# ReLU-squared attention and token/channel mixer: the first batch's transposes move to other PSUM banks, one score tile moves to VectorE, and one pair of DMA transposes moves a round later

## The chip, the core and the metric

The kernel runs on one core of a Trainium2 chip. The metric is the device time of one execution in microseconds (us). The engines are TensorE (PE; its weight loads are PEld), VectorE (DVE), ScalarE (ACT), GpSimd (POOL) and SyncE (SP). In this kernel SP only issues DMAs, and POOL issues the loads, copies a few small things and builds one constant.

## The reference

For 8 batches, 12 heads, 448 tokens and a head width of 64:

```
scores = q @ k.T / 8
attn   = max(scores, 0)**2 / 448
x      = (attn @ v), heads side by side          # 8 x 448 x 768
h      = max(x.T @ w_tok1, 0) @ w_tok2           # over tokens, 448 -> 256 -> 448
u      = x + h.T
out    = u + max(u @ w_ch1, 0) @ w_ch2           # over channels, 768 -> 1536 -> 768
```

Inputs and output are float32. The kernel computes in bf16 with float32 sums.

## The kernel before

**The unit of work** is a group of four heads, numbered i = 0 to 23, three to a batch (`DB` = 3). For each group:

- `load_four` (L73) loads q, k and v; POOL's queue casts them to bf16.
- `transposes(i)` (L127) makes q and k head-major: 56 small transposes on PE into PSUM, then one or two copies to SBUF (`qkT`). With place "att" both halves lie in one slot of the score tiles' pool and are copied by one VectorE instruction of 1792 elements per partition (L152). With place "acc" they lie in the banks acc0 and acc1, with one copy of 896 elements each (L155).
- `scores(i, c)` (L159) for c = 0 to 6: four 64x64 matmuls into a score tile of 128 x 896 float32, then a ReLU on ScalarE (L174) that writes the bf16 tile `at`. The pool `ps_att` has two slots, so a score tile waits until the ReLU of the tile two before has read its slot.
- `square` (L178) squares waiting `at` tiles on VectorE (L181), all but the last `keep`.
- `values(i, cs)` (L183) multiplies the squared tiles with v into acc0 and acc1; `values_out` (L202) moves the sums to `xT`, half on VectorE (L211), half on ScalarE (L207) where `split` is set.
- `x_back(i)` (L223) transposes `xT` to `x_sb`: for i < 8 on PE and by a copy (L246), from i = 8 on by a DMA transpose on SP's queue (L228).
- `token1(i)` (L250) and `token2(i)` (L266) are the token mixer. With `early`, token2's results lie in the pool `ps_mm`, whose tag "bank" has two buffers that go round; then VectorE adds `xT` (L286) and writes `uT`.

The channel mixer follows by batches: `channel1` (L320), `channel2` (L358), whose result is added to `u_sb` on VectorE (L373) and stored from SP's queue (L385). `u_sb` is made by `u_back` (L303), two DMA transposes for each group on SP's queue (L309).

**The order is written out by hand.** Every engine runs its own instructions strictly in the order in which the program issues them, and waits are only put where data or buffers ask for them. PSUM is full: `ps_att` two slots of two banks each, acc0, acc1, and two "bank" buffers.

**The first batch** (L461 to L490) loops over i = 0, 1, 2 and within it over c = 0 to 6. Parts of the group before are laid between the score tiles: values of i-1 at c = 0, 1, 2, token2 of i-2 at c = 1 and 2, x_back of i-1 at c = 4 (into a "bank" buffer, copied by ScalarE), the transposes of the next group at c = 3 (i = 0) or c = 5 (into a score slot), values of i at c = 5 and 6, token1 of i-1 at c = 6. `keep_clock` (L431) issues matmuls on zeros into `warm_ps`, which was taken from "bank" at the very start, in i = 0 and in the first part of i = 1. There is no channel work yet to fill PE with.

**The second batch's first group** (i = 3, L494 to L523) is written out line by line and ends the first batch's last group: squares, values, scores, token2 of 1, x_back of 2, token1 of 2, and so on. From L526 on, all groups run in one loop in which `fill` (L410) lays channel work between the parts.

**u_back's order.** `u_later` (L297) holds the groups whose `uT` is done. At i = 7 the first three are issued (L574 to L577), held back by small POOL copies (`hold_back`, L314). At i = 8 the loop at L545 issues all groups below i - 1 = 7, that is 3, 4, 5 and 6: eight DMA transposes. At i = 9 `x_back(8)`, the first by DMA, comes ahead of `u_back(7)` in program order, and so in SP's queue.

Of the kernel before, what the change touches and what calls it, by code (L numbers as in the profile page):

```python
# [9 lines left out]
FP32 = mybir.dt.float32  # L10
BF16 = mybir.dt.bfloat16
AF = mybir.ActivationFunctionType
ALU = mybir.AluOpType
# [3 lines left out]
def kernel(  # L17
# [11 lines left out]
    nc = tc.nc  # L29

    B, H, S, D = q.shape
# [6 lines left out]
    DB = H // 4  # L38
# [17 lines left out]
    ps_acc = ctx.enter_context(tc.tile_pool(name="ps_acc", bufs=1, space=bass.MemoryType.PSUM))  # L56
    ps_mm = ctx.enter_context(tc.tile_pool(name="ps_mm", bufs=2, space=bass.MemoryType.PSUM))
# [69 lines left out]
    def transposes(i, place="acc", split=False):  # L127
        sb = attn.tile([128, 2, 2, S], BF16, name="qkT")
        if place == "att":
            both = ps_att.tile([128, 2, 1024], BF16, tag="att", name="qkT_ps")  # L130
            parts = [both[:, r] for r in range(2)]
        else:
            parts = [ps_acc.tile([128, 1024], BF16, tag=f"acc{r}", name="qkT_ps1") for r in range(2)]
        for w in (1, 0) if i == 0 else (0, 1):
            src = raws.pop((i, "qk"[w]))
            for c in range(QC):
                at = w * S + c * 64
                for r in range(2):
                    h = slice(64 * r, 64 * (r + 1))
                    for g in range(2):  # L140
                        nc.tensor.matmul(  # L141
                            parts[r][64 * g : 64 * (g + 1), at : at + 64],
                            lhsT=src[h, g, c, :],
                            rhs=ident[h, h],
                            is_transpose=True,
                            start=True,
                            stop=True,
                            skip_group_check=True,
                        )
        qkT[i] = sb  # L150
        if place == "att":
            nc.vector.tensor_copy(sb.rearrange("n r w t -> n r (w t)"), both[:, :, : 2 * S])  # L152
            return
        for r in range(2):
            (nc.scalar.copy if split and r == 0 else nc.vector.tensor_copy)(  # L155
                sb[:, r].rearrange("n w t -> n (w t)"), parts[r][:, : 2 * S]
            )

    def scores(i, c):  # L159
        sb = qkT[i]  # L160
        ps = ps_att.tile([128, 2, 512], FP32, tag="att", name="sc_ps")
        for r in range(2):
            for g in range(2):
                h = slice(64 * g, 64 * (g + 1))
                nc.tensor.matmul(  # L165
                    ps[64 * r : 64 * (r + 1), g, :S],
                    lhsT=sb[h, r, 1, c * 64 : (c + 1) * 64],
                    rhs=sb[h, r, 0, :],
                    start=True,
                    stop=True,  # L170
                    skip_group_check=True,
                )
        at = attn.tile([128, 2, S], BF16, name="at", bufs=12)
        nc.scalar.activation(at, ps[:, :, :S], AF.Relu)  # L174
        squares.append(at)
        at2[i, c] = at

    def square(keep=0):  # L178
        while len(squares) > keep:
            at = squares.pop(0)  # L180
            nc.vector.tensor_tensor(out=at, in0=at, in1=at, op=ALU.mult)  # L181
# [81 lines left out]
        nc.scalar.activation(r1, ps, AF.Relu)  # L263
        r1_tiles[i] = r1

    def token2(i, early=False, rs=(0, 1)):  # L266
        b, d = divmod(i, DB)
        if d == 0 and b % 2 == 0 and 0 in rs:
            uT_tiles[b // 2] = mix.tile([128, NP, 2 * S], BF16, name="uT_sb")
        r1 = r1_tiles[i]  # L270
        off = (b % 2) * S
        if early:
            parts = {r: ps_mm.tile([128, 512], FP32, tag="bank", name="h_ps1") for r in rs}
        else:
            parts = {r: ps_acc.tile([128, 512], FP32, tag=f"acc{r}", name="h_ps") for r in rs}
        for r in rs:
            for j in range(JC):
                nc.tensor.matmul(  # L278
                    parts[r][:, :S],
                    lhsT=r1[:, j, r * 128 : (r + 1) * 128],  # L280
                    rhs=wt2[:, j, :],
                    start=(j == 0),
                    stop=(j == JC - 1),
                )
        for r in rs:
            nc.vector.tensor_tensor(  # L286
                out=uT_tiles[b // 2][:, 2 * d + r, off : off + S],
                in0=parts[r][:, :S],
                in1=xT[b % 2][:, 2 * d + r, :S],
                op=ALU.add,  # L290
            )
        if 1 in rs:
            u_later.append(i)
# [3 lines left out]
    u_later = []  # L297
# [130 lines left out]
    for i in range(9):  # L428
        nc.tensor.matmul(warm_ps, lhsT=warm[:, :128], rhs=warm, start=True, stop=True)

    def keep_clock(n):  # L431

        for m in range(n):
            for r in range(2):
                h = slice(64 * r, 64 * (r + 1))
                nc.tensor.matmul(
                    warm_ps[h, :], lhsT=warm[h, :64], rhs=warm[h, :],
                    start=True, stop=True, skip_group_check=True,
                )
# [15 lines left out]
    load_four(3, "v")  # L455


    keep_clock(2)
    transposes(0, "acc", split=True)
    keep_clock(3)  # L460
    for i in range(DB):  # L461
        for c in range(QC):
            scores(i, c)
            if i == 0:
                keep_clock(0 if c == 3 else 1 if c > 4 else 2)
            if i == 1 and c < 4:
                keep_clock(1)
            square(keep=1)
            if c < 3 and i > 0:
                values(i - 1, (4 + c,))  # L470
                if c == 2:
                    values_out(i - 1, split=True)
            if c in (1, 2) and i > 1:
                token2(i - 2, early=True, rs=(c - 1,))
            if c == 3 and i == 0:
                transposes(1, "att")
            if c == 4 and i > 0:
                x_back(i - 1, copy=nc.scalar.copy)
            if c == 5:
                if i > 0:  # L480
                    transposes(i + 1, "att")
                values(i, (0, 1))
            if c == 6:
                if i > 0:
                    token1(i - 1)
                values(i, (2, 3))
        if i == 1:
            load_four(4)
        if i == 2:
            load_four(5)  # L490
            load_wc1(1, 2)


    i = DB  # L494
    square()
    values(i - 1, (4, 5, 6))
    values_out(i - 1, split=True)
    scores(i, 0)
    token2(i - 2, early=True)
    x_back(i - 1, place="acc0")  # L500
    scores(i, 1)
    token1(i - 1)
    square(keep=1)
# [22 lines left out]
    for i in range(DB + 1, ND + 2):  # L526
        slow = i <= 2 * DB
        if i == 2 * DB + 1:
            rate[0] = (EC * C1 + NT * C2) / DB
        if i < ND:  # L530
            scores(i, 0)
            scores(i, 1)
        if 0 <= i - 1 < ND:
            values(i - 1, range(QC))
            values_out(i - 1)
        if i < ND:
            scores(i, 2)
        if i - 1 < XDMA:
            fill(1 / 3, least=1)
        if 0 <= i - 1 < ND:  # L540
            x_back(i - 1)
        if i > 2 * DB + 1:
            if i == 2 * DB + 2:
                hold_back(1, x_tiles[i - 1][:1, 0, 0, :1])
            while u_later and u_later[0] < i - 1:  # L545
                u_back(u_later.pop(0))
        if i + PRE < ND:
            if i - 1 >= XDMA:
                nc.gpsimd.tensor_copy(gate, x_tiles[i - 1][:1, 1, 3, 127:])  # L549
            load_four(i + PRE)  # L550
        if i == 5:
            load_wc2(1, 2)
        square()
        if i - 1 >= XDMA:
            fill(1 / 3)
        if i < ND:
            scores(i, 3)
            scores(i, 4)
        if i + 1 < ND:
            transposes(i + 1)  # L560
        square()
        if not slow:
            fill(2 / 9)
        if 0 <= i - 1 < ND:
            token1(i - 1)
        fill(1 / 3 if slow else 1 / 9, least=1)
        if i < ND:
            scores(i, 5)
            scores(i, 6)
        if 0 <= i - 1 < ND:  # L570
            token2(i - 1)
            if (i - 1) % DB == DB - 1:
                channel_work((i - 1) // DB)
            if i == 2 * DB + 1:  # L574
                hold_back(0, uT_tiles[1][:1, 0, :1])
                for _ in range(DB):
                    u_back(u_later.pop(0))  # L577
        square()
        fill(1 / 3, least=1 if slow else 0)
# [32 lines left out]
```

## Time and profile before

| | |
|---|---|
| median of 7 runs | 381.34 us (379.6 to 382.7) |
| the profiled execution's own time | 381.02 us |
| its span, first to last instruction | 379.2 us |
| PE busy | 364.9 us (96%) |
| ACT busy | 213.4 us (56%) |
| DVE busy | 206.5 us (54%) |
| POOL busy | 100.3 us (26%) |
| granted TensorE clock, mean | 1.000 |

A row of a timeline holds the start, the length, the engine, the line in the kernel, the operation, what it writes and reads, how many instructions are merged, and, in square brackets, how long the engine had sat idle and what ended that. Lengths of neighbours on one engine overlap a little: on VectorE and ScalarE the next instruction starts about 0.1 us before the end of the one before. A merged group of matmuls is as long as from its first start to its last modelled end; the next group starts before that. The chain of waits is followed back from a last instruction through whatever released each step.

### The profile page before, as it was taken

Reading aid. Unit: us, or ns where it says so; the run is one execution under the profiler, and the core shown is the slowest. Engines: PE = TensorE matmul, PEld = TensorE weight load, DVE = VectorE, ACT = ScalarE, POOL = GpSimd, SP = SyncE. Lnnn points to the kernel's source line nnn. Section 1 sums busy time; section 2 is a strip of 40 time slices with the busy share of each in tenths; the row PEclk is TensorE's granted clock in tenths of the full one; section 3 lists DMA queues with packets and bytes.
Section 4 is the critical chain, followed back from the end, with each engine's and each line's share of the span. In section 5 each row is a group of like instructions: output and inputs, shape, how many; then the busy total and the mean of one; then the engine's idle time right before and its main releaser. Section 6 shows DMA issues by size and latency. Waiting matters only on the chain.

```text
span 379.2 us, 10082 instructions
## 1 busy us (share of the span) xinstructions
PE 364.9 (96%) x4335; PEld 200.6 (53%) x4335; DVE 206.5 (54%) x371; ACT 213.4 (56%) x297; POOL 100.3 (26%) x186
## 2 busy tenths in 40 slices
PE   7878999999979999999999999999999999999995
PEld 3444455555545554555555654555545654555563
DVE  2886688764566575465555664466555664121021
ACT  4996888877434457755676247654676446412400
POOL 8976347312312321421312304303300000000000
PEclk9999999999999999999999999999999999999999
DMA  8999999913998866947745798648451434333024
GB/s 150 119 161 197 177 206 188 165 25 74 110 170 154 149 143 113 112 77 153 130 86 74 128 163 132 102 70 171 87 106 23 90 93 92 57 69 85 0 61 107
DMA packets 69325, 43.30 MB, mean 114 GB/s; under 512 B 43360, under 2 KB 65824, under 8 KB 69280
## 3 DMA queue, kind: packets, MB, share of 16 engines
q0 software_dynamic: 24416, 21.47, 40.0%
q1 hardware_dynamic: 44560, 20.75, 25.8%
q8 instruction: 34, 0.56, 0.6%
q10 hardware_dynamic: 304, 0.43, 0.4%
q14 instruction: 11, 0.09, 0.1%
HBM read 43.38 MB, written 11.01 MB: 143 GB/s over the span
## 4 chain that ended last, share of the span: by engine, by line
PE 87%; DVE 4%; DMA 3%; ACT 3%; POOL 2%; issue 1%; POOLq 0%; ACTq 0%; SPq 0%
PE m_ps L327 28%; PE m_ps L366 28%; PE sc_ps L165 9%; PE acc_ps L193 8%; PE t_ps L255 6%; PE h_ps L278 5%; DMA x_sb<-xT 3%; PE qkT_ps L141 2%; ACT at L174 2%; DVE uT_sb L286 1%; DVE at L181 1%; POOL q_raw L83 1%; PE m_ps L345 1%; DMA wt<-in_moe_w_tok_dram 1%; PE x_ps L237 1%
## 5 line engine op out<-in xcount | busy, mean ns | idle before, releaser
L174 ACT ACTIVATE at<-sc_ps 128x896 bf16<-128x896 f32 x168 | 145.1, 921 | 59.3 <-PE sc_ps L165 59.1
L327 PE MATMUL m_ps<-uT_sb,wc 128*128 128x448 bf16 x564 | 115.6, 353 | 0.2 <-DVE uT_sb L286 0.2
L366 PE MATMUL m_ps<-wc,r_sb 128*128 128x384 bf16 x672 | 115.2, 326 | 0.0
L181 DVE TENSOR_TENSOR at<-at 128x896 bf16<-128x896 bf16 x168 | 97.3, 622 | 7.1 <-ACT at L174 7.1
L366 PEld LDWEIGHTS <-r_sb 128*128 128x128 bf16 x672 | 64.3, 98 | 45.6 <-issue 3.9
L334 ACT ACTIVATE r_sb<-m_ps 128x448 bf16<-128x448 f32 x94 | 51.1, 543 | 60.1 <-PE m_ps L327 59.8
L327 PEld LDWEIGHTS <-wc 128*128 128x128 bf16 x564 | 53.3, 98 | 49.8 <-issue 4.3
L373 DVE TENSOR_TENSOR out_sb<-m_ps,u_sb 128x384 f32<-128x384 f32 x56 | 31.1, 556 | 62.0 <-PE m_ps L366 61.0
L165 PE MATMUL sc_ps<-qkT 64*64 64x448 bf16 x672 | 52.7, 360 | 2.9 <-ACT at L174 2.3
L286 DVE TENSOR_TENSOR uT_sb<-h_ps,xT 128x448 bf16<-128x448 f32 x48 | 27.8, 619 | 39.4 <-PE h_ps L278 39.3
L211 DVE TENSOR_SCALAR xT<-acc_ps 128x448 bf16<-128x448 f32 x45 | 26.1, 620 | 34.9 <-PE acc_ps L193 34.9
L193 PE MATMUL acc_ps<-at,v_raw 64*64 64x448 bf16 x672 | 38.6, 349 | 0.0
L549 POOL COPY gate<-x_sb 1x1 bf16<-1x1 bf16 x12 | 2.4, 199 | 127.4 <-DMA x_sb<-xT 127.4
L83 POOL DMA_DIRECT2D q_raw<-in_q_dram x48 | 29.0, 615 | 17.4 <-DMA wc<-in_moe_w_ch_dram 14.0
L83 POOL DMA_DIRECT2D v_raw<-in_v_dram x48 | 29.4, 637 | 10.4 <-DMA wc<-in_moe_w_ch_dram 5.2
L165 PEld LDWEIGHTS <-qkT 64*64 64x64 bf16 x672 | 15.6, 105 | 30.7 <-issue 26.6
L155 DVE COPY qkT<-qkT_ps 128x896 bf16<-128x896 bf16 x39 | 22.6, 619 | 14.6 <-PE qkT_ps L141 14.6
L83 POOL DMA_DIRECT2D k_raw<-in_k_dram x46 | 28.1, 632 | 1.4 <-DMA k_raw<-in_k_dram 0.9
L255 PE MATMUL t_ps<-x_sb,wt 128*128 128x256 bf16 x192 | 25.0, 273 | 3.3 <-DMA x_sb<-xT 2.5
L263 ACT ACTIVATE r_sb<-t_ps 128x512 bf16<-128x512 f32 x24 | 14.3, 597 | 21.8 <-PE t_ps L255 21.7
L193 PEld LDWEIGHTS <-v_raw 64*64 64x64 bf16 x672 | 20.2, 107 | 12.1 <-issue 0.8
L255 PEld LDWEIGHTS <-wt 128*128 128x128 bf16 x192 | 18.2, 98 | 9.1 <-DMA x_sb<-xT 3.4
(40 smaller groups left out, 125.4 us busy)
## 6 DMA issues: line engine op xcount, KB each, us to landing
out_dram<-out_sb SPq DMA_DIRECT2D x54, 192.0 KB, 3.5
q_raw<-in_q_dram POOLq DMA_DIRECT2D x48, 112.0 KB, 4.4
v_raw<-in_v_dram POOLq DMA_DIRECT2D x48, 112.0 KB, 5.6
k_raw<-in_k_dram POOLq DMA_DIRECT2D x46, 112.0 KB, 5.7
wc<-in_moe_w_ch_dram POOLq DMA_DIRECT2D x4, 1152.0 KB, 10.5
u_sb<-uT_sb SPq DMA_TRANSPOSE x48, 2.8
x_sb<-xT SPq DMA_TRANSPOSE x16, 3.3
k_first<-in_k_dram SPq DMA_DIRECT2D x1, 224.0 KB, 3.5
```

The costliest lines, as they stand in the source:

```text
L83: eng.dma_start(out=dst[64 * r : 64 * (r + 1)].rearrange("p g c d -> p g (c d)"), in_=src[b, h0 : h0 + 2].rearrange("g (p c) d -> p g (c d ...
L165: nc.tensor.matmul(ps[64 * r : 64 * (r + 1), g, :S], lhsT=sb[h, r, 1, c * 64 : (c + 1) * 64], rhs=sb[h, r, 0, :], start=True, stop=True, s ...
L174: nc.scalar.activation(at, ps[:, :, :S], AF.Relu)
L181: nc.vector.tensor_tensor(out=at, in0=at, in1=at, op=ALU.mult)
L193: nc.tensor.matmul(ps[r][64 * g : 64 * (g + 1), :S], lhsT=v_raw[h, g, c, :], rhs=at[h, g, :], start=(c == 0), stop=(c == QC - 1), skip_gro ...
L211: nc.vector.tensor_scalar(out=xT[b % 2][:, 2 * d + r, :S], in0=ps[r][:, :S], scalar1=float(alpha2), scalar2=None, op0=ALU.mult,)
L255: nc.tensor.matmul(ps[:, j, :], lhsT=wt1[:, c, j * 128 : (j + 1) * 128], rhs=x_sb[:, :, c, :], start=(c == 0), stop=(c == 3),)
L286: nc.vector.tensor_tensor(out=uT_tiles[b // 2][:, 2 * d + r, off : off + S], in0=parts[r][:, :S], in1=xT[b % 2][:, 2 * d + r, :S], op=ALU.add,
L327: nc.tensor.matmul(ps[:, :S], lhsT=wc1[:, g, e * 128 : (e + 1) * 128], rhs=uT[:, g, off : off + S], start=(g == 0), stop=(g == CC - 1),)
L334: nc.scalar.activation(r2[:, e, off : off + S], ps[:, :S], AF.Relu)
L366: nc.tensor.matmul(ps[:, :HN], lhsT=r2[:, e, t * 128 : (t + 1) * 128], rhs=wc2[:, e, cols], start=(e == 0), stop=(e == EC - 1),)
L373: nc.vector.tensor_tensor(out=o[:, cols].rearrange("n (g d) -> n g d", d=128), in0=ps[:, :HN].rearrange("n (g d) -> n g d", d=128), in1=u_ ...
```

## The change

1. `transposes(1)`, `transposes(2)` and `transposes(3)` use two "bank" buffers of `ps_mm` instead of one score slot; their copy becomes two copies of 896 elements on VectorE (the line of L155) instead of one of 1792 (L152). `transposes(4)` stays in a score slot.
2. After `transposes(1)`, `warm_ps` is taken anew from "bank", since its old buffer went to the transposes.
3. Score tile (0, 2) gets its ReLU from VectorE instead of ScalarE (a maximum with 0), and is then squared on VectorE as all are.
4. Values of a group come one score tile later: chunks 0 and 1 at c = 6 instead of c = 5, then (2, 3), (4, 5) and (6) at c = 0, 1, 2 of the next i; at i = 3, chunks 2 to 5 come ahead of the last `square`.
5. `x_back(0)` and `x_back(1)` go to acc0 instead of "bank"; the copy of `x_back(0)` moves from ScalarE to VectorE. At i = 3, `x_back(2)` is put between the two additions of `token2(1)`.
6. At i = 8 the loop issues `u_back` only up to group 5; group 6's two DMA transposes come at i = 9, behind `x_back(8)`.

```diff
-            parts = [ps_acc.tile([128, 1024], BF16, tag=f"acc{r}", name="qkT_ps1") for r in range(2)]
+            pool, tags = (ps_acc, ("acc0", "acc1")) if place == "acc" else (ps_mm, ("bank", "bank"))
+            parts = [pool.tile([128, 1024], BF16, tag=tag, name="qkT_ps1") for tag in tags]
...
-        nc.scalar.activation(at, ps[:, :, :S], AF.Relu)
+        if alone:
+            nc.vector.tensor_scalar(
+                out=at, in0=ps[:, :, :S], scalar1=0.0, scalar2=None, op0=ALU.max
+            )
+        else:
+            nc.scalar.activation(at, ps[:, :, :S], AF.Relu)
...
         for r in rs:
+            if r == 1 and between:
+                between()
             nc.vector.tensor_tensor(
                 out=uT_tiles[b // 2][:, 2 * d + r, off : off + S],
...
     for i in range(DB):
         for c in range(QC):
-            scores(i, c)
+            scores(i, c, alone=(i, c) == (0, 2))
...
             if c < 3 and i > 0:
-                values(i - 1, (4 + c,))
+                values(i - 1, ((2, 3), (4, 5), (6,))[c])
...
             if c == 3 and i == 0:
-                transposes(1, "att")
+                transposes(1, "bank")
+                warm_ps = ps_mm.tile([128, 512], FP32, tag="bank", name="warm_ps")
             if c == 4 and i > 0:
-                x_back(i - 1, copy=nc.scalar.copy)
-            if c == 5:
-                if i > 0:
-                    transposes(i + 1, "att")
+                x_back(i - 1, place="acc0", copy=nc.scalar.copy if i > 1 else None)
+            if c == 5 and i > 0:
+                transposes(i + 1, "bank")
+            if c == 6:
                 values(i, (0, 1))
-            if c == 6:
                 if i > 0:
                     token1(i - 1)
-                values(i, (2, 3))
...
     i = DB
+    values(i - 1, (2, 3, 4, 5))
     square()
-    values(i - 1, (4, 5, 6))
+    values(i - 1, (6,))
     values_out(i - 1, split=True)
     scores(i, 0)
-    token2(i - 2, early=True)
-    x_back(i - 1, place="acc0")
+    token2(i - 2, early=True, between=lambda: x_back(DB - 1, place="acc0"))
...
-            while u_later and u_later[0] < i - 1:
+            while u_later and u_later[0] < max(i - 1 - (i == 2 * DB + 2), 0):
                 u_back(u_later.pop(0))
```

More of the change, by code (lines that the diff above doesn't have):

```diff
@@ L157, in transposes, with scores @@
             )
-    def scores(i, c):
+    def scores(i, c, alone=False):
         sb = qkT[i]
@@ L264, in token1, with token2 @@
         r1_tiles[i] = r1
-    def token2(i, early=False, rs=(0, 1)):
+    def token2(i, early=False, rs=(0, 1), between=None):
         b, d = divmod(i, DB)
@@ L429, with keep_clock @@
         nc.tensor.matmul(warm_ps, lhsT=warm[:, :128], rhs=warm, start=True, stop=True)
-    def keep_clock(n):
+    def keep_clock(n, warm_ps):
         for m in range(n):
@@ L455 @@
     load_four(3, "v")
-    keep_clock(2)
+    keep_clock(2, warm_ps)
     transposes(0, "acc", split=True)
-    keep_clock(3)
+    keep_clock(3, warm_ps)
     for i in range(DB):
         for c in range(QC):
-            scores(i, c)
+            scores(i, c, alone=(i, c) == (0, 2))
             if i == 0:
-                keep_clock(0 if c == 3 else 1 if c > 4 else 2)
+                keep_clock(0 if c == 3 else 1 if c > 4 else 2, warm_ps)
             if i == 1 and c < 4:
-                keep_clock(1)
+                keep_clock(1, warm_ps)
             square(keep=1)
             if c < 3 and i > 0:
-                values(i - 1, (4 + c,))
+                values(i - 1, ((2, 3), (4, 5), (6,))[c])
                 if c == 2:
```

## The prediction

> **What bounds the kernel now.** I read the slices of the page first, then the chain of waits up to 36 us, then every idle stretch of PE, then SP's queue around the one long one. Score tile c of group i is written (i, c).
>
> ```profile
> PE   7878999999979999999999999999999999999995
> ...
> ACT  4996888877434457755676247654676446412400
> ...
> PEclk9999999999999999999999999999999999999999
> ```
>
> From the fifth slice on (about 38 us) PE is full, but for the slice near 110 us; in the first four ScalarE is at 8 and 9 tenths too, and the clock is full. So a gain must come from the first 35 us or from the hole near 110 us. All other work is PE work in a row, and carries an earlier start unchanged to the end.
>
> ```profile
> 27.59 1.07 ACT x_sb L246
> 28.66 0.83 ACT at L174
> 29.49 0.04 issue
> 29.53 0.38 PE sc_ps L165 x4
> 29.91 0.98 PE t_ps L255 x8
> ...
> 32.68 1.16 DVE uT_sb L286 x2
> 33.84 0.61 DVE x_sb L246
> 34.44 0.04 issue
> 34.49 1.03 PE t_ps L255 x8
> ```
>
> These are pieces of the chain: start, length, engine and line. The front is a relay of ScalarE and VectorE, which PE waits for. The last link that matters is the copy of x_sb at 33.84, since token1(2) at 34.49 waits for it; after that PE has no idle stretch above 0.4 us until the hole.
>
> ```profile
> 84.15 21.89 SPq L309 DMA_TRANSPOSE u_sb<-uT_sb  x14
> 106.14 1.18 SPq L385 DMA_DIRECT2D out_dram<-out_sb  x2
> 107.42 1.32 SPq L228 DMA_TRANSPOSE x_sb<-xT  x1
> ```
>
> ```profile
> 104.11 1.16 DVE L211 TENSOR_SCALAR xT<-acc_ps 128x448 bf16<-128x448 f32 x2 [1.27 <-PE acc_ps L193]
> ```
>
> ```profile
> 111.85 1.05 PE L255 MATMUL t_ps<-x_sb,wt 128*128 128x256 bf16 x8 [2.50 <-DMA x_sb<-xT]
> ```
>
> That is the hole: SP issues 14 transposes of u and two stores ahead of the transpose of x(8), whose data xT was ready at 104.11 + 1.16 = 105.27; it is issued at 107.42, lands at 111.81, and PE has been idle 2.50 us.
>
> **The first 35 us, part by part.** Steps come from the timeline: score matmul to its ReLU 0.43 (12.64 to 13.07), ReLU to ReLU 0.81, length 0.92; a freed slot to the next matmul 0.05; VectorE back to back 0.53 for a square or a copy of 896; four matmuls of scores or values take 0.19 of PE, two pairs of keep_clock 0.41.
>
> The VectorE ReLU of 128x896 float32 from PSUM is not in the trace. L211 (448 float32) takes 0.62 and L155 (896 bf16) 0.62, so I read 896 float32 like L152's 1792 bf16: 1.09. Below it could be 0.62, above twice L211, 1.24.
>
> *Group 0.* Before, the transposes of group 1 held a score slot from 10.79 until their copy ended at 12.58, and ScalarE stood still 0.49 twice. After: ReLU (0,2) on VectorE 9.68 to 10.77 (behind the square of (0,0), 9.15 + 0.53); (0,3) on ScalarE 10.41 instead of 10.61; transposes 10.19 to 10.87 (their loads landed by 10.02); (0,4) finds its slot free at 10.77, so its ReLU starts at 11.25 instead of 12.03, 0.78 ahead. But VectorE is now in arrears: squares at 10.69 and 11.22, copies 11.75 to 12.37 and 12.28 to 12.90. The new warm_ps lies in the buffer of the first copy, so the keep_clock behind (0,4) waits until 12.42, and behind it on PE stand (0,5) and everything after. (0,5) comes at 12.42 + 0.41 = 12.83, its ReLU at 13.26 against 13.07. **The gain of 0.78 becomes a loss of 0.2.** The later values move PE work only, which has room; (1,4) is at 18.52 against 18.29.
>
> *Group 1.* x_back(0)'s copy (L246, 1.10) leaves ScalarE, so (1,5) starts 19.33 instead of 19.98. VectorE gets it instead: square (1,3) 18.72, copy 19.25 to 19.94 (0.69, its own row of L246), square (1,4) 19.86, copies of group 2 at 20.39 to 21.01 and 20.92 to 21.54. token1(0) now needs the buffer of the first copy: 21.06 against 21.37. ReLU (2,0), behind token1's, is at 22.85 against 23.16: **0.3 ahead**.
>
> *Group 2.* Equal steps keep 0.29 up to (2,5), 28.19 against 28.48. Then (2,6), which waited 0.71 for the copy of the transposes in its slot, has a slot since (2,4) ended: ReLU 29.01 against 29.96. The next latest are x_sb's copy on ScalarE (ends 28.37), which values(2) in acc0 now waits for, and the first qkT copy (28.06 to 28.68), which token1(1) waits for: it starts about 28.80 against 29.85. **0.95 to 1.05 ahead.**
>
> *Group 3.* Values (2,6) wait for their square (29.96 to 30.58) and run at 30.63; xT 31.03 against 32.00; first addition of token2(1) 31.60 against 32.68. x_sb's copy now goes between the additions: PE's transposes are done at 32.48, copy 32.50 to 33.18 against 33.75 to 34.43. token1(2) starts at 33.23 against 34.49: **1.25 ahead**, 0.3 of it from the place between the additions. The second addition (33.10 to 33.72) is needed by channel1_begin at 34.5 only, whose weights landed at 31.60.
>
> Loads do not undo it: the nearest, k of group 4, landed at 35.05 and is needed at 38.9.
>
> One row speaks against group 1:
>
> ```profile
> 20.03 1.09 DVE L152 COPY qkT<-qkT_ps 128x1792 bf16<-128x1792 bf16 x1
> 21.04 1.17 DVE L181 TENSOR_TENSOR at<-at 128x896 bf16<-128x896 bf16 x1
> ```
>
> The square at 21.04 took 1.17 instead of 0.62; POOL's two copies (L105) ran from 20.02 to 21.72. The copy out of PSUM beside them took its usual time. In the changed order the square of (1,4) meets that stretch ahead of the copies. It starts 0.16 before POOL does, so I charge nothing; if it is held as that row was, 0.55, group 1 ends 0.24 behind and the front gains 0.7; held for both copies, it gains nothing. [...] Bounds of the front: a loss of 0 and, with a 0.62 ReLU on VectorE, a gain of 1.7. **I take 1.25.**
>
> **The hole at 110 us.** With group 6 moved behind x(8), SP's twelfth transpose ends at 102.6; the two stores follow (their data was there at 99.6) to 103.9, and x(8) is issued when xT is ready, 105.3 instead of 107.4. If its landing takes 3.3 as the median does, it lands at 108.6, before PE runs dry at 109.35: gain 2.5. But the transposes issued from 96.4 on landed only at 105.06 to 107.05, about 0.5 apart: loads that POOL issued at 94.5 shared the engines until 104.5. If x(8) stands behind that backlog, only two transposes fewer lie ahead of it: gain 0.9. With 4.4 to landing, as now, it lands at 109.7 to 110.2. **I take a gain of 1.7**, near that row. [...] The four u transposes then end at about 112 against 111.5 and the next stores start there: x(9) is issued at 121, out of reach; group 6's u_sb belongs to batch 2, whose output comes long after.
>
> **Sum.** 381.02 - 1.25 - 1.7 = 378.1 for the profiled execution. The median of the runs shown is 0.3 higher, which is less than their scatter; I leave the forecast at 378.1. A measurement of this kernel can tell about 0.5% (1.9 us) from no change.
>
> **Rivals.**
> - *The transfer stays late.* x(8) lands no earlier, because stores and backlog lie ahead. For it: landings lag issues by 8 us at 97 us. Against: the backlog ends by 107.5. Gain 1.25 to 2.15: **379.3**. Chance 0.17.
> - *VectorE takes ScalarE's place in front.* It is busy 8.17 of 9.5 us from 25 to 34.5, and token1 now waits for its copies. Front 0 to 0.4, hole 1.7: **379.1**. Chance 0.15.
> - *Neither pays:* **380.6**. Chance 0.07.
> - *Slower: the clock falls.* PE gets a new idle stretch, 11.2 to 12.4 us. Up to 34.5 us PE is busy 17.7 of the 22 us that follow; at half clock (the first 4 us ran at that, 0.43 a matmul of 512) that is 35 us, 13 late at most, 2 if it recovers within 4 us: with the gains, between 380 and 391, middle **385.6**. It decides only if the stretch exceeds what the clock bears, and the 2.50 us at 109.35 left it at 1.00. Chance 0.06.
>
> The forecast has 0.55, with 376.8 to 379.0 as its own range. The range: from both upper bounds (381.02 - 1.7 - 2.5 = 376.8) to neither paying, 380.6. Faster by over 0.5% (below 379.1) are the forecast nearly whole, 0.53, and under half of the first two rivals, 0.13: 0.66. Slower 0.06, the rest 0.28.
>
> **What would show it.** After: VectorE's ReLU near 1.1 us at 9.7; a PE wait of about 1.2 us ahead of keep_clock near 12.4, put down to a VectorE copy; token1(0) near 21.1, token1(1) near 28.8, token1(2) near 33.2; x(8) issued 2 us after its xT's start at the latest, with PE idle under 1 us ahead of token1(8); clock 1.00. Wrong: token1(2) later than 34, a square over 1 us near 20, or a hole of 2 us still there.

## The result and the profile after

| | before | changed |
|---|---|---|
| median | 380.44 us (379.60 to 382.70, 31 runs) | 377.80 us (377.22 to 378.43, 12 runs) |
| the profiled execution's own time | 381.02 us | 378.43 us |
| its span | 379.2 us | 376.6 us |
| PE idle ahead of token1(8) | 2.50 us | 0.80 us |

The ratio of the mean times is 0.9916, with an interval of [0.9897, 0.9935]: the changed kernel is faster by 0.65 to 1.0%. The forecast was 378.1, range 376.8 to 380.6.

Where the time went is read from the starts of token1, since all PE work between them has the same length in both:

| start of | before | changed | difference |
|---|---|---|---|
| token1(0) | 21.37 | 21.24 | -0.13 |
| token1(1) | 29.85 | 29.44 | -0.41 |
| token1(2) | 34.49 | 33.88 | -0.61 |
| token1(7) | 95.84 | 95.24 | -0.60 |
| token1(8) | 111.85 | 109.55 | -2.30 |
| token1(16) | 229.01 | 226.44 | -2.57 |
| end | 379.15 | 376.58 | -2.57 |

So the front gave 0.61, the hole 1.70, and the wait ahead of group 16 another 0.27. From the page of the changed kernel, the slices:

```profile
span 376.6 us, 10084 instructions
...
PE   8888999999999999999999999999999999999995
...
ACT  4887888877434457745676347654576446412400
...
PEclk9999999999999999999999999999999999999999
```

The 7 in PE's twelfth slice (104 to 114 us) has become a 9, and the clock stays full. From the changed kernel's chain of waits between 18 and 36 us (start, length, engine and line):

```profile
14.92 6.94 DMA wt_nat<-in_moe_w_tok_dram
21.86 0.05 issue
21.91 2.34 POOL wt L105 x2
24.25 0.04 issue
24.29 0.35 PE h_ps L284
...
27.83 1.05 ACT x_sb L252
28.89 0.04 issue
28.93 0.57 PE acc_ps L199 x8
...
33.14 0.70 DVE x_sb L252
33.84 0.04 issue
33.88 1.03 PE t_ps L261 x8
```

Two things are to be seen. The last link before token1(2) is again a copy of x_sb, now between the additions of token2(1). But the chain no longer comes through the relay of ScalarE and VectorE in groups 0 and 1: it comes from the load of w_tok2 (`wt_nat`) and POOL's two copies of it (L105); the second matmul of token2(0), at 24.29, waits for the second copy.

SP's queue of the changed kernel:

```profile
83.54 19.05 SPq L317 DMA_TRANSPOSE u_sb<-uT_sb  x12
102.68 1.18 SPq L393 DMA_DIRECT2D out_dram<-out_sb  x2
104.69 1.29 SPq L234 DMA_TRANSPOSE x_sb<-xT  x1
106.03 6.17 SPq L317 DMA_TRANSPOSE u_sb<-uT_sb  x4
```

VectorE's row that makes xT(8), and PE's row that waits for x(8):

```profile
103.51 1.16 DVE L217 TENSOR_SCALAR xT<-acc_ps 128x448 bf16<-128x448 f32 x2 [1.27 <-PE acc_ps L199]
```

```profile
109.55 1.05 PE L261 MATMUL t_ps<-x_sb,wt 128*128 128x256 bf16 x8 [0.80 <-DMA x_sb<-xT]
```

xT is ready at 103.51 + 1.16 = 104.67, and the transpose is issued 0.02 later: the queue costs nothing any more. It lands at 109.50, 4.8 us after its issue, and PE still waits 0.80.

### The profile page after: what moved, and what is told of

It is laid out like the page before. It is cut to its first block, busy times and chain, and to the rows that moved or that the text cites. A ratio compares the mean times of both kernels' runs of the same rounds, so it can differ in the third digit from the quotient of the medians.

```text
span 376.6 us, 10084 instructions
## 1 busy us (share of the span) xinstructions
PE 365.8 (97%) x4335; PEld 201.3 (53%) x4335; DVE 208.3 (55%) x376; ACT 211.5 (56%) x295; POOL 101.0 (27%) x186
## 4 chain that ended last, share of the span: by engine, by line
PE 88%; DMA 5%; POOL 3%; DVE 2%; issue 1%; ACT 1%; POOLq 0%; ACTq 0%
PE m_ps L335 29%; PE m_ps L374 28%; PE sc_ps L166 9%; PE acc_ps L199 8%; PE t_ps L261 5%; PE h_ps L284 5%; PE qkT_ps L142 2%; DMA wt_nat<-in_moe_w_tok_dram 2%; DMA q_raw<-in_q_dram 1%; DMA x_sb<-xT 1%; PE x_ps L243 1%; POOL q_raw L83 1%; PE m_ps L353 1%; POOL wt L105 1%; DVE uT_sb L294 1%
## 5 line engine op out<-in xcount | busy, mean ns | idle before, releaser
L156 DVE COPY qkT<-qkT_ps 128x896 bf16<-128x896 bf16 x45 | 26.0, 619 | 15.2 <-PE qkT_ps L142 15.2
L199 PEld LDWEIGHTS <-v_raw 64*64 64x64 bf16 x672 | 20.3, 107 | 13.1 <-issue 1.7
L284 PE MATMUL h_ps<-wt,r_sb 128*128 128x448 bf16 x96 | 22.6, 355 | 0.5 <-POOL wt L105 0.5
```

Source lines behind the costliest of these rows:

```text
L199: nc.tensor.matmul(ps[r][64 * g : 64 * (g + 1), :S], lhsT=v_raw[h, g, c, :], rhs=at[h, g, :], start=(c == 0), stop=(c == QC - 1), skip_gro ...
L284: nc.tensor.matmul(parts[r][:, :S], lhsT=r1[:, j, r * 128 : (r + 1) * 128], rhs=wt2[:, j, :], start=(j == 0), stop=(j == JC - 1),)
```

## The experiments

**The theory** was that two independent gains add up: the front (parts 1 to 5), now held back by keep_clock's wait in group 0 and then by w_tok2; and the hole (part 6). **The rivals**: that only one of them pays, that the VectorE ReLU or the place between the additions does the work of the front, and for the rest of the hole that either the transfers ahead of x(8) or those behind it keep it late.

The front is compared by the start of token1(2) counted from the first ReLU of the same profile, since executions start up to 0.7 us apart. It is 26.29 us before and 25.49 in the first profile of the changed kernel. The median of each kernel stands beside that of before, run beside it.

**1. Part 6 alone** (before, with the one line):

```diff
-            while u_later and u_later[0] < i - 1:
+            while u_later and u_later[0] < max(i - 1 - (i == 2 * DB + 2), 0):
```

> The kernel before with part 6 alone: group 6's two transposes of u come behind x(8). Theory A (two gains, each in its place): the wait of PE ahead of token1(8) falls from 2.50 us to 0.8 or less, the start of token1(2) stays where it was (34.2 to 34.8), and the time is 1.7 to 2.2 us under that of before. Rival B (the front gives nothing, its 0.60 us in the profile is the scatter of the loads): the time is that of the changed kernel, 377.8. Rival C (moving the transposes only moves the wait): the wait turns up at token1(9) or at a store, and the time is that of before.

379.27 against 380.36, ratio 0.9962 [0.9944, 0.9979]. token1(2) stays at 34.49; x(8) is issued at 105.33 and lands at 110.18; PE waits 0.87 instead of 2.50. The hole's gain is 1.6 us in the profile, without the front, but 1.1 in the medians. The profiled execution of before, 381.02, lies 0.6 above the median of its kernel, and the next experiment shows that the hole is not always 2.50 us long.

**2. Parts 1 to 5 alone** (the changed kernel with that line undone).

> The changed kernel with part 6 taken back: the front alone. Theory A: token1(2) starts at 33.2 to 34.0 instead of 34.49, the wait ahead of token1(8) is 2 us or more again, and the time is 0.6 to 1.2 us under that of before. Rival B: no gain that can be told from before, within 0.3 us. If the scatter of the times of before (379.6 to 382.7) comes from the hole, this kernel scatters as widely, and the one with part 6 alone does not.

378.93 against 380.36, ratio 0.9968 [0.9944, 0.9992]. token1(2) is 24.92 after the first ReLU, 1.37 earlier than before. Medians of 1.1 and 1.4 below before for the parts stand beside 2.7 for both in the runs beside them: the gains add up, within 0.2.

One expectation failed: the wait ahead of token1(8) was to be 2 us or more, since part 6 is undone. SP's queue and PE in the profile, the fastest of the twelve executions (377.97):

```profile
104.45 1.34 SPq L234 DMA_TRANSPOSE x_sb<-xT  x1
```

```profile
109.03 1.05 PE L261 MATMUL t_ps<-x_sb,wt 128*128 128x256 bf16 x8 [1.13 <-DMA x_sb<-xT]
```

Here xT was ready at 102.65 + 1.16 = 103.81, and the queue of 14 transposes and two stores made x(8) only 0.64 late; in the profile of before it was 2.15 late. So the hole that part 6 closes is not always 2.50 us long; whether the earlier front or the execution makes the difference is not shown. The other expectation held: this kernel scatters as widely as before (377.97 to 381.60), and part 6 alone does not (378.93 to 379.76).

**3. The changed kernel again**, unedited.

> The changed kernel once more, for a second profile of it and as the measure for the others of this chip: 377.2 to 378.4. The first profile had the front 0.60 us ahead, with PE waiting 0.46 us for the reordered token weights (landed at 21.86 instead of 19.96). If that is the scatter of the loads, the weights land at another time here, and where they land by 20.5 token1(2) starts 1.0 us or more ahead of before's 34.49; if the change itself makes them late, they land at 21.5 to 22.2 again.

377.66 against 380.36, ratio 0.9925 [0.9900, 0.9949]. In this execution w_tok2 landed at 20.30 instead of 21.86, and token1(2) came 24.92 after the first ReLU instead of 25.49. So the first profile shows the front 0.57 short, and it is one and the same program: the load's landing differs between executions. In the four profiles with an unaltered front in which w_tok2 landed by 20.3 (this one, 2, 4 and 10) token1(2) stands at 24.91 or 24.92.

**4. Group 5's transposes moved behind x(8) too**, so that SP has nothing left to issue ahead of it.

```diff
-            while u_later and u_later[0] < max(i - 1 - (i == 2 * DB + 2), 0):
+            while u_later and u_later[0] < max(i - 1 - 2 * (i == 2 * DB + 2), 0):
```

> The changed kernel with group 5's two transposes of u behind x(8) as well. If x(8) lands late because of what stands ahead of it in SP's queue (theory A), it lands about 1 us earlier, the remaining wait of 0.80 us ahead of token1(8) goes, and the time falls by 0.6 to 0.9 us under the changed kernel. If its own latency or the loads beside it set the landing, the wait stays near 0.8 and the time the same. If the four transposes more behind it push the next stores and x(9), a wait of up to 1 us appears ahead of token1(9) instead.

377.75 against 380.36, ratio 0.9928 [0.9903, 0.9952]: no different from experiment 3. SP is done with its stores at 99.4, x(8) is issued at 103.92 and still takes 4.76 us. What stands ahead of x(8) is not why it lands late.

**5. No keep_clock at (0, 4)**, so that its wait for the copy goes (four matmuls on zeros are left out).

```diff
-                keep_clock(0 if c == 3 else 1 if c > 4 else 2, warm_ps)
+                keep_clock(0 if c in (3, 4) else 1 if c > 4 else 2, warm_ps)
```

> The changed kernel without the keep_clock behind score tile (0, 4): four matmuls on zeros less, the computation is whole. In three profiles the ReLU of (0, 5) starts 5.07 to 5.08 us behind that of (0, 0) (before: 4.87), because PE waits 1.05 to 1.22 us for VectorE's copy ahead of that keep_clock. Theory A (this wait is what eats the gain in group 0): (0, 5) follows at about 3.9, (0, 6) at 4.85 instead of 5.89, and the lead of up to 1.0 us lasts to token1(2) (23.9 to 24.3 behind the first ReLU instead of 24.92), if the reordered token weights are there in time; time 0.5 to 1.0 us under the changed kernel. Rival B (the next wait is as late: copies on VectorE, loads, the token weights): (0, 5) comes earlier, token1(2) does not, and the time is the same within 0.3 us. Rival C: without these matmuls the clock falls in the front and the time rises by 1 us or more.

377.10 against 380.32, ratio 0.9906 [0.9870, 0.9942]. ReLU (0, 5) is 3.87 after the first ReLU instead of 5.07, and token1(0) 11.83 instead of 12.85. Of that 1.0 us, token1(2) keeps 0.16 (24.76): w_tok2 landed at 21.74, and PE waited 0.46 for POOL's copies. The wait is real, and the weights hide what its removal brings.

**6. ReLU (0, 2) on ScalarE again.**

```diff
-            scores(i, c, alone=(i, c) == (0, 2))
+            scores(i, c)
```

> The changed kernel with the ReLU of (0, 2) back on ScalarE. Theory A (VectorE's arrears hold the keep_clock, and ScalarE's relief is lost there): the first copy of group 1's q and k ends about 0.45 us earlier, and the ReLU of (0, 5) follows the first one at 4.6 us instead of 5.07; this lead of 0.45 stays to token1(2), and the time falls by 0.3 to 0.5 us. So part 3 by itself would be a loss. Rival B (ScalarE bounds group 0, so the tile on VectorE is a gain): (0, 5) comes at 5.07 or later, and the time rises by 0.2 to 0.8 us.

377.42 against 380.32, ratio 0.9901 [0.9868, 0.9933]. (0, 5) comes at 4.63 instead of 5.07 and token1(0) at 12.48 instead of 12.85: VectorE's ReLU made group 0 later, since it delays the copies that keep_clock waits for. token1(2) is at 25.04, with w_tok2 late (20.81). The VectorE tile is no source of the gain.

**7. x_back(2) behind both additions of token2(1)** (part of 5 undone).

```diff
-    token2(i - 2, early=True, between=lambda: x_back(DB - 1, place="acc0"))
+    token2(i - 2, early=True)
+    x_back(i - 1, place="acc0")
```

> The changed kernel with x_back(2) behind both additions of token2(1), as before the change. Theory A: x_sb's copy comes 0.3 us later, token1(2) at 25.2 us behind the first ReLU instead of 24.92, time 0.3 us over the changed kernel. Rival B: PE's transposes end so late that the second addition fits ahead of the copy anyway; token1(2) and the time stay.

378.02 against 380.32, ratio 0.9930 [0.9908, 0.9952]; token1(2) at 25.16 instead of 24.92: the place is worth 0.24.

**8. transposes(2) and (3) in a score slot again.**

```diff
-                transposes(i + 1, "bank")
+                transposes(i + 1, "att")
```

> The changed kernel with the transposes of groups 2 and 3 back in a score slot (group 1's stay in the token banks). Theory A (the slot taken from the score tiles is what delays them: score tile (2, 6) then has to wait for the ReLU of (2, 5) instead of (2, 4)): PE waits 0.4 to 0.9 us ahead of (1, 6) and (2, 6) again, token1(2) starts 25.6 to 25.9 us behind the first ReLU instead of 24.92, and the time is 0.6 to 1.0 us over the changed kernel. Rival B (the front's gain comes from the later values and the moved x_sb copies, not from the slot): token1(2) and the time stay within 0.3 us.

378.92 against 380.62, ratio 0.9947 [0.9927, 0.9967]; token1(2) at 25.88, 0.96 later than 24.92. This is the largest part of the front's gain. The row of PE that shows it, score tile (2, 6) in this kernel, and ScalarE's row in the changed kernel with (2, 5) and (2, 6) back to back:

```profile
28.78 0.38 PE L166 MATMUL sc_ps<-qkT 64*64 64x448 bf16 x4 [1.09 <-ACT at L180]
```

```profile
28.73 1.79 ACT L180 ACTIVATE at<-sc_ps 128x896 bf16<-128x896 f32 x2
```

With the transposes in one of the two slots, score tiles take turns in the other, and (2, 6) waits for the ReLU of (2, 5).

**9. w_tok2 loaded earlier, no keep_clock at (0, 4)**: the load moves ahead of group 2's q and k.

```diff
     load_wt1()
+    load_wt2()
...
-    load_wt2()
...
-                keep_clock(0 if c == 3 else 1 if c > 4 else 2, warm_ps)
+                keep_clock(0 if c in (3, 4) else 1 if c > 4 else 2, warm_ps)
```

> The kernel without the keep_clock behind (0, 4), and with the load of the second token weights moved ahead of the loads of group 2's q and k and group 1's v. Without the keep_clock alone, token1(0) started 1.0 us earlier (11.83 behind the first ReLU instead of 12.86), but token1(2) only 0.16, and PE waited 0.46 us for POOL's copies of these weights, which landed at 21.74. Theory A (the weights had become the next bound): they land before 17 us, that wait is gone, token1(2) starts 23.9 to 24.1 behind the first ReLU, time 0.9 to 1.2 us under the changed kernel. Rival B (VectorE or the other loads are as late): token1(2) stays at 24.7 or more and the time within 0.3 us of the kernel without the keep_clock alone (377.1).

378.32 against 380.62, ratio 0.9946 [0.9920, 0.9973]. The weights landed at 13.71 and nothing waits for them; yet token1(2) is at 24.92, no better than without either edit. VectorE's row of the square of (1, 4), and PE's of token1(0), in this kernel:

```profile
18.70 1.63 DVE L187 TENSOR_TENSOR at<-at 128x896 bf16<-128x896 bf16 x1
```

```profile
20.92 1.03 PE L261 MATMUL t_ps<-x_sb,wt 128*128 128x256 bf16 x8 [1.51 <-DVE qkT L156]
```

POOL's copies now run from 18.12 to 19.84, beside that square: it takes 1.63 instead of 0.62, the copies of qkT behind it are late, and PE waits 1.51 instead of 0.49. The theory that early weights free the front falls; the long square beside POOL's copies took their place.

**10. Nothing right behind x(8)**: groups 6 and later are issued from i = 10 on.

```diff
-            while u_later and u_later[0] < max(i - 1 - (i == 2 * DB + 2), 0):
+            while u_later and u_later[0] < (2 * DB if i <= 2 * DB + 3 else i - 1):
```

> The changed kernel with no transpose of u behind x(8) at i = 9 (groups 6, 7 and 8 go at i = 10). x(8) landed 4.76 us after its issue even where the queues were empty when it was issued, while x(10) takes 3.3. Theory A (the u transposes that SP issues right behind x(8) share the engines with it): x(8) lands 3.3 to 3.6 us after its issue, the wait ahead of token1(8) falls below 0.2 us, and the time falls by 0.6 to 0.9 us. Rival B (something else, such as the 16 KB of instruction code that is fetched at about that time): it still takes 4.5 us or more, and wait and time stay. In either case six transposes at once at i = 10 may hold up x(10) and make a new wait there.

377.18 against 380.32, ratio 0.9910 [0.9878, 0.9942]. x(8) is issued at 103.63 and lands at 106.67, after 3.04 us, and PE does not wait at all. x(10), now the next behind six transposes of u that SP issues from 118.23 to 126.1, takes 4.62, and token1(9) to token1(10) takes 14.59 instead of 14.41. I read this as the transposes behind x(8) making it late. Experiment 12 took that reading away.

**11. Everything together**: the edits of 9, and u in two portions.

```diff
-            while u_later and u_later[0] < max(i - 1 - (i == 2 * DB + 2), 0):
+            while u_later and u_later[0] < (2 * DB if i <= 2 * DB + 3 else 2 * DB + 2 if i == 2 * DB + 4 else i - 1):
```

> Both edits of the run before, and no transposes of u behind x(8): groups 6 and 7 go at i = 10, group 8 with 9 at i = 11. If the gains add (no keep_clock wait and early weights 0.9 to 1.0, the rest of the hole 0.6 to 0.9), the time is 375.7 to 376.3 us, 1.2% under before, with no wait of PE over 0.3 us from 34 us on. If the transposes put off hold up x(10) or x(11), a wait of up to 0.5 us appears ahead of token1(10) or token1(11) and the time is 376.3 to 376.8.

377.27 (376.14 to 378.99) against 380.62, ratio 0.9908 [0.9874, 0.9941]. There is no hole (x(8) takes 3.57), but the profiled execution, one of the two slowest of six, lost more in front than was won: token1(2) at 27.03. VectorE, POOL and PE in this kernel:

```profile
17.60 2.73 DVE L187 TENSOR_TENSOR at<-at 128x896 bf16<-128x896 bf16 x1 [0.37 <-ACT at L180]
```

```profile
18.10 1.73 POOL L105 COPY wt<-wt_nat 128x448 bf16<-128x448 bf16 x2
```

```profile
20.99 0.96 PE L199 MATMUL acc_ps<-at,v_raw 64*64 64x448 bf16 x8 [2.18 <-DVE x_sb L252]
22.05 1.86 PE L261 MATMUL t_ps<-x_sb,wt 128*128 128x256 bf16 x8
```

And its stretches (bounds, length, busy us of PE, PEld, DVE, ACT and POOL with counts, granted clock, DMA share, GB/s):

```profile
19.00:21.00 2.00, 0.01 (x4) 0.01 (x4) 2.00 (x3) 1.00 (x2) 2.00 (x4) 0.99 1.19 183
21.00:24.40 3.40, 3.29 (x24) 1.63 (x27) 2.60 (x5) 0.45 (x1) 3.40 (x7) 0.51 1.06 148
24.40:30.00 5.60, 4.98 (x116) 2.33 (x107) 4.56 (x9) 5.56 (x9) 0.52 (x2) 1.00 1.19 205
```

The square of (1, 3) took 2.73 instead of 0.62 and ended at 20.33, behind both copies of POOL (19.83). PE then stood idle for 2.18 us, and after that the granted clock was 0.51 for 3.4 us: token1's eight matmuls took 1.86 instead of 1.03.

**12. The two gains without the early weights**: no keep_clock at (0, 4), u in two portions as in 11, w_tok2 where the changed kernel loads it.

> The two edits that paid, together: no keep_clock behind (0, 4), and no transpose of u behind x(8) (groups 6 and 7 at i = 10, group 8 with 9 at i = 11); the token weights stay where the changed kernel loads them, so POOL's copies do not meet VectorE's squares ahead of token1(0). If the gains add, 0.5 us each under the changed kernel's 377.7: 376.4 to 377.0 us, no wait above 0.3 us ahead of token1(8), no stretch of half clock after the first 8 us, and a scatter of the times below 1.5 us. If the lead in the front makes POOL's copies late for token2(0), the front gives 0.2 and the time is 376.8 to 377.2.

376.66 (376.13 to 377.07, 4 runs) against 380.27, ratio 0.9898 [0.9882, 0.9915]: the lowest median of all. token1(2) stands at 24.61, the earliest of all. But the hole is not gone, and SP's queue is that of experiment 10 around x(8). First experiment 10, then this one:

```profile
103.63 1.23 SPq L234 DMA_TRANSPOSE x_sb<-xT  x1
105.70 6.58 SPq L393 DMA_DIRECT2D out_dram<-out_sb  x4
```

```profile
103.49 1.23 SPq L234 DMA_TRANSPOSE x_sb<-xT  x1
105.56 7.33 SPq L393 DMA_DIRECT2D out_dram<-out_sb  x4
```

```profile
108.16 1.05 PE L261 MATMUL t_ps<-x_sb,wt 128*128 128x256 bf16 x8 [0.61 <-DMA x_sb<-xT]
```

In both, nothing stands behind x(8) for 2 us, and it took 3.04 us in one and 4.63 in the other. So the transposes behind x(8) are not the cause, or not all of it.

**What the records of the DMA engines show instead.** Beside the kernel's own queues the page lists the queue "q8 instruction": packets of 16 KB, by the queue's name program code. The changed kernel's DMA answer for 107.0 to 109.5 us (40 slices, in tenths of all engines and in GB/s) holds one of them:

```profile
DMA  9765567999997200100000000100000010000000
GB/s 467 148 143 131 115 103 147 184 205 238 188 213 172 49 4 1 1 0 0 0 0 0 0 0 8 8 8 8 8 8 12 8 12 8 8 0 0 0 0 0
...
q8 instruction: 1, 0.02, 3.7%
```

The code packet runs from 107.05 to 108.53. All but 24 of the 1408 packets of x(8) and of the u transpose behind it (1024 and 384) have started by 107.9; the 24 go on only when the code packet is over, in a trickle of 8 GB/s, to 109.2. That is one of 16 engines' share of the u transpose, so one engine seems to have stood behind the code packet. x(8) counts as landed at 109.50, 1.0 us after the code packet's end, though its own packets had started by 107.36; why it takes that long is not shown. In experiment 12 the code packet runs from 106.04 to 106.92. x(8)'s 1024 packets of 256 bytes, and 30 of the 32 packets of 4 bytes that end it, have started by 106.07; the last two start at 106.90, and x(8) lands at 108.11. In experiment 10 the code packet starts at 106.47, when x(8)'s last packet had been over for 0.26 us, and x(8) lands at 106.67. The DMA answer of experiment 10 for 103.6 to 106.3 us has none:

```profile
DMA  9900000000000000005999999999999999997300
...
q1 hardware_dynamic: 1088, 0.31, 55.6%
...
x_sb<-xT SPq DMA_TRANSPOSE x1, 3.0
```

I laid the code packets over all 196 transposes of x that the fourteen profiles record with their landing. 59 had none near (from 1 us ahead of the issue to 5 us behind it): all of these took 3.16 to 3.33 us. Of 39 with one that starts 1.1 to 3.03 us after the issue, 35 took 4.5 to 5.1; the other four, 3.04 to 3.57, include x(8) of experiments 10 and 11, in which it starts behind the last packet. Only 3 of the other 98, with one earlier or later, took over 4.3. **So the rest of the hole goes with a code packet that falls into the transfer.** No experiment moved a code packet by itself: the connection is read from the records, not made by an edit, and the 35 late cases are not 35 independent ones. They lie at three places of the program, x(8), x(11) and x(16), profile after profile.

## Why the prediction was right, point by point

**The sum.** For the profiled execution it was 381.02 - 1.25 - 1.7 = 378.1. It measured 381.02 - 0.61 - 1.70 - 0.27 = 378.44, and its own time is 378.43. The forecast is 0.3 above the median of 377.80 and in its own range; both gains were real and added up (experiments 1 and 2). That the sum came so close is in part luck: in this profile the front fell 0.64 short, and group 16 gave 0.27 that was not forecast. In the medians the two parts are worth 1.4 and 1.1, against 1.25 and 1.7 in the sum.

**Group 0: right.** VectorE's ReLU and PE's wait in the changed kernel:

```profile
9.88 1.08 DVE L176 TENSOR_SCALAR at<-sc_ps 128x896 bf16<-128x896 f32 x1
```

```profile
12.62 0.40 PE L444 MATMUL warm_ps<-warm 64*64 64x512 bf16 x2 [1.05 <-DVE qkT L156]
```

1.08 us against 1.09, and counted from the first ReLU the wait ends at 4.23 against 4.22, and ReLU (0, 5) comes at 5.07 against 5.06. The loss that this wait makes of a gain was the right reading (experiment 5: 1.0 us at token1(0)).

**Group 1: right in sum.** token1(0) came 12.85 after the first ReLU, against 12.86.

**"Loads do not undo it": this step failed.** I looked at the loads of group 4 and not at w_tok2, which token2(0) needs. POOL before, then the changed kernel's VectorE and POOL:

```profile
20.02 1.70 POOL L105 COPY wt<-wt_nat 128x448 bf16<-128x448 bf16 x2 [1.21 <-DMA wt_nat<-in_moe_w_tok_dram]
```

```profile
21.64 1.86 DVE L187 TENSOR_TENSOR at<-at 128x896 bf16<-128x896 bf16 x2
23.75 0.97 DVE L187 TENSOR_TENSOR at<-at 128x896 bf16<-128x896 bf16 x1 [0.25 <-ACT at L180]
```

```profile
21.91 2.33 POOL L105 COPY wt<-wt_nat 128x448 bf16<-128x448 bf16 x2 [2.33 <-DMA wt_nat<-in_moe_w_tok_dram]
```

In before the copies started at 20.02 and ended at 21.72, 1.9 us ahead of token2(0)'s first matmul at 23.61. Here they started at 21.91, took 2.33 instead of 1.70, and PE waited 0.46 at 24.29. That is 0.57 of the front in this execution and nothing in experiment 3, where the load was on time. With it token1(1) came at 29.44 instead of about 28.8, and token1(2) at 33.88 instead of 33.2.

**The held square: charged nothing, cost something.** The two squares at 21.64 took 1.86 instead of 1.15 and the next 0.97 instead of 0.62, beside POOL's copies. The prediction saw only VectorE held, by 0.55 or for both copies: with the load late, the POOL copies stretched too (1.11 and 1.28 against 0.88). That a square with a lead of 0.16 us over POOL pays nothing was my estimate, and no run shows it. In experiment 11 the square's record starts at 17.60, ahead of POOL's 18.10, and it still took 2.73, to 20.33, while POOL's copies ended at 19.83. So even a lead of 0.50 did not spare a square.

**Group 2: the size right, the releaser wrong.** The prediction had (2, 6) of before wait 0.71 for the copy of the transposes in its slot. The row of before names ScalarE:

```profile
29.53 0.38 PE L165 MATMUL sc_ps<-qkT 64*64 64x448 bf16 x4 [0.71 <-ACT at L174]
```

It waited for the ReLU of (2, 5) in the other slot, which ended at 28.48 + 1.00 = 29.48. The slot that the transposes hold makes two tiles take turns in one. Where the weights were on time (experiment 3), token1(1) came 20.47 after the first ReLU, 1.18 ahead of before, against 0.95 to 1.05; with both slots given back (experiment 8) it is at 21.48, so 1.01 of this lead is theirs.

**Group 3: right.** 0.24 for the place between the additions (experiment 7) against 0.3, and 1.37 for the whole front where the weights were on time, against 1.25.

**The hole: right size in this profile, wrong reason for it.** SP was as worked out: twelve transposes, two stores, no wait for the queue. The landing 4.4 us after the issue was put down to a backlog. Experiment 4 emptied the queue ahead and x(8) took 4.76; the records put the delay beside a code packet. That 1.7 came out is therefore luck in part: it was chosen between 0.9 and 2.5 by one row, and against a hole of 2.50 us that is not there at that length in every execution (experiments 1 and 2). The row that I chose, 4.4 from before, had such a packet too, at 0.69 us after its issue; the median of 3.3 was that of transfers without one. The 0.27 at group 16 goes with the same: x(16) took 5.22 in before and 4.88 in the changed kernel, with a code packet in both.

**The rivals.** Neither the late transfer (379.3) nor VectorE in ScalarE's place (379.1) came about. The clock did not fall: 12 runs lie within 1.2 us, at a mean granted clock of 0.997 to 1.000, and the page shows nines. But in experiment 11 it did fall in the front, and the rival's deciding point was set wrongly. I took 2.50 us of idle PE as borne, since the granted clock behind it was 1.00 in before; in experiment 11 2.18 us was followed by 3.4 us at 0.51. So the length of the idle stretch alone does not tell the two apart, and what does is not shown. The half clock that the rival gives the first 4 us is read from the length of the matmuls there (634 ns in the median of the nine of 128x512, 379 in the shortest); the granted clock on record for 0 to 4 us is 1.00.

**Before loses clock in some executions.** Its times spread over 3.1 us. The mean granted clock is on record for 67 of its runs, those beside the experiments. In 14 of them it is 0.993 to 0.996, and these are the 14 longest, 381.97 to 382.71; in the other 53 it is 0.997 or more, and the longest of them took 381.31. One stretch of 3.4 us at half clock, as in experiment 11, would take 1.7 us of clock, 0.0045 of 380 (an estimate), which fits. With part 6 undone (experiment 2) it was 3 of 12 runs; with part 6 it was none of 12 in experiment 1, and none of the changed kernel's 12 and 6. So part 6 does more than one profile shows: the long executions are gone with it. Lower clock came back in experiments 8 (1 of 11), 9 (4 of 11) and 11 (2 of 6), which have part 6. In 9 and 11 PE waits 1.51 and 2.18 us ahead of token1(0).

**What stays open.** No profile of before or of experiments 2, 8 and 9 fell on a run with a lower clock, so where in it the clock falls is not shown; that it falls behind the hole is argued from part 6 alone. Parts 2 and 4, group 1's transposes and the move of x_back(0) and x_back(1) were not undone one by one; experiments 7 and 8 account for 1.2 of the front's 1.37. Nor is it shown whose code the packets bring, or why x(10) of experiment 10 was late with its code packet only at 4.39 us behind the issue.

## What to carry to other kernels

When a chain is shortened, ask for every operand of the next stage what arrives last, weights included, and look at how much that arrival differs between executions before relying on the margin. A PSUM slot that is lent from a pool of two costs the turns that the tiles must then take in the other one (0.96 us here). Close an idle stretch of PE even where one profile shows the clock bearing it (here it stayed at 1.00 behind 2.50 us in one profile and was 0.51 behind 2.18 us in another), and read the granted clock of every run, not only of the profiled one. Before moving DMAs out of a late transfer's way, look whether the delay lies in the queue at all (with the queue empty ahead of it, x(8) still took 4.76 us).

## What the runs showed of the hardware

- **Transfers with a code packet in their middle were late.** The queue "q8 instruction" carries 34 packets of 16 KB, 0.56 MB, in the changed kernel. A DMA transpose of 128 x 1024 bf16 took 3.16 to 3.33 us without one of them near, and 4.5 to 5.1 in 35 of 39 cases with one in its middle.
- **A VectorE square beside two POOL copies in a row ended only after both**: 2.73 us for a square of 0.62 (experiment 11), 1.63 in experiment 9. In the first profile of the changed kernel both sides were longer beside each other: 1.86 for two squares and 0.97 for the next, 1.11 and 1.28 for POOL's copies of 0.88.
- **The granted clock was 0.51 for 3.4 us after 2.18 us of idle PE** (experiment 11), and 1.00 after 2.50 us in the profile of before. Of 67 other runs of before, 14 had a lower mean clock (0.993 to 0.996), and were the 14 longest.
- **The landing of one load moved by 1.6 us** between two executions of the same kernel (w_tok2 at 21.86 and 20.30).
